# Attention and expert routing on one core: new order of steps in a slot, five experts in two passes, key copies on ScalarE, scatters as units end

One Trainium2 chip, one core. The metric is the device time of one execution in microseconds (us). The kernel before takes 208.21 us (median of 3; 207.79 to 211.42). All stamps below are us from the start of the profiled span of the run named. "Granted clock" is the share of full TensorE clock that the profile records; half clock is a record of 0.50. A clock window is one of the stretches of 3.41 us at whose borders these records change.

## The reference

Attention over 4 batches, 8 heads, 768 tokens and head size 64; three heads are causal, five see four first keys and a window of 64. Its output, 3072 tokens by 512, goes to a layer of 8 experts, of which each token uses one or none:

```python
out = x.copy()
do_compute = x @ w_skip > 0
logits = xc @ w_gate                  # xc = x[do_compute]
e_idx = argmax(logits); gate_w = softmax(logits)[e_idx]
for e in range(8):
    h = maximum(xc[mask] @ w1[e], 0)  # 512 -> 1024
    y[mask] = gate_w * (h @ w2[e])    # 1024 -> 512
out[do_compute] = xc + y
```

## The kernel before

Each batch has six slots. A slot mixes score products of batch b (`C`, `H6`, `X`), transposes of q and k (`T`), the attention product of batch b-1 for 128 tokens (`"o"`), and for earlier tokens the transposes of x and the gate scores (`"x"`). In TensorE's program they stand in this order.

```python
def ready(g):                       # this is "x"
    xt(g - 1)                       # 4 transposes of x, copied to SBUF
    gates(g - 2)                    # 4 products with 9 columns, into av's bank

return (
    (C(0), "x", "o", C(1), T(1)),
    (C(2), "x", "o", T(2), C(3)),
    (C(4), "x", "o", C(5), H6(0)),
    (H6(2), "x", "o", T(3), lambda: after_t(b), H6(4)),
    ...
)
...
    if g in (NT + 1, 2 * NT + 1):   # after the second slot of batches 2 and 3
        routing = route(g - NT - 1) # starts by reading the gate scores in av
```

After the last batch a table of slots is made, and GpSimd gathers the tokens of each expert (`gather`), loads weights and scatters results, all in its program order. Experts 0 to 3 run as two units of up to 128 tokens, in two passes; the others as one unit of up to 256.

```python
FB = 4
units = [(e, (t,)) for t in range(T2) for e in range(FB)]
units += [(e, (0, 1)) for e in range(FB, E)]
for n in range(len(units)):
    ...                             # up product, down product
    if n == FB - 1: load_half(FB + 2, 0)
    elif n == FB:   load_half(FB + 2, 1); load_half(FB + 3, 0)
    elif n > FB:
        if n == FB + 1: load_half(FB + 3, 1)
        scatters()                  # loads first, then the scatters
```

The softmax here doesn't subtract the row's maximum and nothing guards it: scores larger than these inputs give would overflow.

## Time and profile before

| | before |
|---|---|
| time, median | 208.21 us |
| profiled span, mean granted TensorE clock | 204.6 us, 0.95 |
| first gather (end of attention and routing) | 109.52 us |
| from first gather to end of span | 95.1 us |

I split the span at the first gather, because all that follows waits for the slot table. The prediction shows the page's lines and the GpSimd timeline.

### The profile page before, as it was taken

The numbers are of one execution on the slowest core, as the hardware profiler recorded it, in microseconds if no ns is written. First come the engines' busy times: TensorE is split into PE (matmuls) and PEld (weight loads), VectorE is DVE, ScalarE is ACT, GpSimd is POOL, SyncE is SP. The second block draws the span as 40 slices with busy tenths as digits, with TensorE's granted clock in tenths as the row PEclk, the third lists the DMA queues.
The fourth block names the chain that finished last, engine by engine and source line by source line (L and its number), as shares of the span: only waits on it lengthen the run. The fifth ranks groups of instructions, "written<-read, shape, count | busy, mean of one in ns | idle before, by whom it ended". The sixth has DMA issues, their size and how long they took to land. (4 is left out here: it accounts for less than half of the span.)

```text
span 204.6 us, 5665 instructions
## 1 busy us (share of the span) xinstructions
PE 163.1 (80%) x2422; PEld 116.7 (57%) x2422; DVE 111.9 (55%) x282; ACT 83.5 (41%) x116; POOL 85.1 (42%) x105
## 2 busy tenths in 40 slices
PE   5898878967788687886898688959988959999900
PEld 1455556746566565664777558648755727657400
DVE  5888877554957849574683626233345344344410
ACT  2067788855874558746121133212322422232000
POOL 8659711421861218412014801687632451145430
PEclk9999999999999999999669889988999999999985
DMA  5999999999899999999999899999999999942010
GB/s 164 174 172 157 180 196 214 222 181 229 139 182 228 240 216 246 225 190 243 215 235 272 222 171 238 208 302 239 239 258 181 208 210 211 278 155 79 23 67 3
DMA packets 53172, 39.97 MB, mean 195 GB/s; under 512 B 27976, under 2 KB 44360, under 8 KB 53136
## 3 DMA queue, kind: packets, MB, share of 16 engines
q0 software_dynamic: 49136, 32.43, 104.2%
q1 hardware_dynamic: 3728, 6.69, 9.7%
q8 instruction: 21, 0.34, 0.6%
q10 hardware_dynamic: 272, 0.39, 0.5%
q14 instruction: 15, 0.12, 0.2%
HBM read 56.66 MB, written 10.49 MB: 328 GB/s over the span
## 5 line engine op out<-in xcount | busy, mean ns | idle before, releaser
L433 POOL CAST x<-x 128x512 f16<-128x512 f32 x17 | 10.7, 627 | 43.3 <-DVE x L426 37.4
L344 ACT ACTIVATE at<-sps 128x1024 f16<-128x1024 f32 (+1 forms) x24 | 21.7, 918 | 11.6 <-PE sps L333 11.1
L685 POOL DMA_INDIRECT out_dram<-xg,idx x16 | 16.0, 1001 | 24.0 <-DVE xg L748 10.6
L731 PE MATMUL mhp<-mxT,w1t 128*128 128x128 f16 (+1 forms) x320 | 24.4, 238 | 0.7 <-ACT mxT L717 0.7
L731 PEld LDWEIGHTS <-w1t 128*128 128x128 f16 x320 | 22.6, 103 | 3.5 <-issue 1.1
L735 DVE TENSOR_SCALAR ht<-mhp 128x512 f16<-128x512 f32 x16 | 11.1, 691 | 23.3 <-PE mhp L731 20.3
L746 PE MATMUL myp<-w2t,ht 128*128 128x512 f16 x96 | 23.6, 380 | 0.0
L748 DVE SCALAR_TENSOR_TENSOR xg<-myp,tab,xg 128x512 f32<-128x512 f32 x16 | 12.0, 751 | 19.6 <-PE myp L746 18.2
L679 POOL DMA_INDIRECT xg<-out_dram,idg x16 | 16.4, 1025 | 10.5 <-DVE tab L536 4.8
L737 ACT ACTIVATE ht<-mhp 128x512 f16<-128x512 f32 x16 | 9.6, 597 | 26.5 <-PE mhp L731 21.1
L383 ACT ACTIVATE ats<-sps 128x1024 f16<-128x1024 f32 (+1 forms) x16 | 12.3, 808 | 14.6 <-PE sps L374 14.6
L746 PEld LDWEIGHTS <-ht 128*128 128x128 f16 x128 | 12.0, 99 | 10.3
L439 PE MATMUL xps<-ident,x 128*128 128x128 f16 (+1 forms) x96 | 12.9, 263 | 6.0 <-ACT qT L302 2.4
L302 DVE COPY kT<-tps 128x768 f16<-128x768 f16 x16 | 15.2, 951 | 3.5 <-PE tps L296 3.5
L333 PE MATMUL sps<-qT,kT 64*128 64x512 f16 (+3 forms) x96 | 15.1, 308 | 0.0
L328 PE MATMUL sps<-tri,idl 64*128 64x128 f16 x144 | 11.4, 221 | 3.3 <-ACT ats L383 2.7
L717 ACT COPY mxT<-mtp 128x512 f16<-128x512 f16 x11 | 6.2, 587 | 17.7 <-PE mtp L714 16.8
L426 DVE TENSOR_TENSOR x<-av,rec 128x512 f32<-128x512 f32 x18 | 12.5, 692 | 1.4
L349 ACT ACTIVATE at<-sps 128x1024 f16<-128x1024 f32 (+1 forms) x12 | 10.8, 916 | 5.0 <-PE sps L333 4.8
L114 POOL DMA_DIRECT2D va<-in_v_dram x8 | 11.4, 1426 | 2.7 <-DMA va<-in_v_dram 1.2
L446 DVE COPY xT<-xps 128x512 f16<-128x512 f16 x17 | 7.6, 446 | 7.2 <-PE xps L439 7.0
L517 POOL TENSOR_TENSOR mv<-ot,vals 128x192 f32<-128x192 f32 (+1 forms) x4 | 2.5, 618 | 21.7 <-DVE ot L511 21.7
(152 smaller groups left out, 341.5 us busy)
## 6 DMA issues: line engine op xcount, KB each, us to landing
out_dram<-x SPq DMA_DIRECT2D x24, 256.0 KB, 5.8
w1t<-in_moe_w_dram POOLq DMA_DIRECT2D x6, 1024.0 KB
w2t<-in_moe_w_dram POOLq DMA_DIRECT2D x6, 1024.0 KB
va<-in_v_dram POOLq DMA_DIRECT2D x8, 384.0 KB
qin<-in_moe_w_dram POOLq DMA_DIRECT2D x2, 1024.0 KB
kin<-in_moe_w_dram POOLq DMA_DIRECT2D x2, 1024.0 KB
qin<-in_q_dram POOLq DMA_DIRECT2D x2, 768.0 KB
kin<-in_k_dram POOLq DMA_DIRECT2D x2, 768.0 KB
```

The lines of the kernel that those rows point to most:

```text
L114: nc.gpsimd.dma_start(out=y[:, x, :D], in_=vr[b, :, x])
L302: eng(t.rearrange("c (p n) -> c p n", n=NT), ps.rearrange("c n p -> c p n"))
L333: nc.tensor.matmul(ps[:, k, x:x + n], kT[b, pr][rows[i], j * P:(j + 1) * P], qT[b, pr][rows[i], q0:q0 + n], start=False, stop=True, skip_g ...
L344: nc.scalar.activation(both[b][:, :, o:o + w], ps[:, :, :w], ACT.Exp, scale=SCALE)
L383: nc.scalar.activation(both[b, pr][:, :, x0:x1], ps[:, :, :x1 - x0], ACT.Exp, scale=SCALE)
L426: nc.vector.tensor_tensor(x.rearrange("p c t d -> p t c d"), avo[:, :, :, :D], rec.unsqueeze(3).to_broadcast([P, 2, 4, D]), op=ALU.mult)
L439: nc.tensor.matmul(ps[:, s], x[:, s * P:(s + 1) * P], ident if x.dtype == FP16 else ident32, is_transpose=True, start=(s == 0), stop=(s == ...
L679: nc.gpsimd.indirect_dma_start(out=xg[e, t], out_offset=None, in_=out[:n, :], in_offset=bass.IndirectOffsetOnAxis(ap=idg[:, t, e:e + 1], a ...
L685: sc = nc.gpsimd.indirect_dma_start(out=out[:, :], out_offset=bass.IndirectOffsetOnAxis(ap=idx[:, t, e:e + 1], axis=0), in_=xg[e, t], in_o ...
L731: nc.tensor.matmul(hp[:, u], wts[e, 0][:, s, (f0 + u) * P:(f0 + u + 1) * P], xts[n][:, s], start=(s == 0 and u == 0), stop=(s == DS - 1 an ...
L746: nc.tensor.matmul(yp, hts[n][:, f, i * P:(i + 1) * P], wts[e, 1][:, f], start=(f == 0), stop=(f == FS - 1))
L748: nc.vector.scalar_tensor_tensor(xg[e, t], yp, tab[:, t, e, 1:2], xg[e, t], ALU.mult, ALU.add)
```

## The change

The intent: put the transposes and gate scores behind the attention product, so that TensorE does not wait for the casts that they need; take half of the key copies from VectorE; load earlier; do the last gate scores between the first units; take five experts in two passes; scatter as units end. The core of the diff (PSUM pools and the unit loop's head are cut):

```diff
-            eng = nc.scalar.copy if name == "qT" and b else nc.vector.tensor_copy
+            eng = nc.scalar.copy if b and (name == "qT" or pr > 1) else nc.vector.tensor_copy
...
-            (C(0), "x", "o", C(1), T(1)),
-            (C(2), "x", "o", T(2), C(3)),
-            (C(4), "x", "o", C(5), H6(0)),
-            (H6(2), "x", "o", T(3), lambda: after_t(b), H6(4)),
-            (X(1, (0,), 0, S), "x", "o", X(2, pair, 0, 512), V(1, 2, 3), X(2, pair, 512, S)),
+            (C(0), "o", C(1), "x", T(1)),
+            (C(2), "o", T(2), C(3), "x"),
+            (C(4), "o", C(5), "x", H6(0)),
+            (H6(2), "o", T(3), lambda: after_t(b), "x", H6(4)),
+            (X(1, (0,), 0, S), "o", X(2, pair, 0, 512), "x", V(1, 2, 3), X(2, pair, 512, S)),
...
         after_o(b)
+        load()
+        load()
...
-    FB = 4
+    FB = 5
...
+        if n > 2:
+            scatters()
         if n == FB - 1:
+            load_half(FB + 1, 0)
+        elif n == FB:
+            load_half(FB + 1, 1)
             load_half(FB + 2, 0)
-        elif n == FB:
+        elif n == FB + 1:
             load_half(FB + 2, 1)
-            load_half(FB + 3, 0)
-        elif n > FB:
-            if n == FB + 1:
-                load_half(FB + 3, 1)
-            scatters()
```

## The prediction

> **What bounds the kernel now.** Times below are us from the start of the profiled span (204.6 us; the timed runs have a median of 208.21). I read the page first, for the busy shares and the slices:

> ```profile
> PE 163.1 (80%) x2422; PEld 116.7 (57%) x2422; DVE 111.9 (55%) x282; ACT 83.5 (41%) x116; POOL 85.1 (42%) x105
> PEclk9999999999999999999669889988999999999985
> DMA  5999999999899999999999899999999999942010
> q0 software_dynamic: 49136, 32.43, 104.2%
> ```

> PE is busy 80% of the span, but the DMA engines are at nine tenths in nearly every slice up to about 180 us, and nearly all of it is one queue, the one GpSimd fills. So there are two full resources, and the end is set by how they interlock. The clock row has dips (6s and 8s): TensorE ran at half clock at 99-106, 116-120 and 136-140.

> Second, the chain of work that ended last, of which I take the pieces after the routing:

> ```profile
> 136.77 10.04 DMA xg<-out_dram,idg
> 147.11 12.61 DMA xg<-out_dram,idg
> 164.60 16.08 DMA out_dram<-xg,idx
> 187.99 6.92 PE myp L746 x32
> ```

> The last gather is issued at 147.1 and lands at 159.7; the chain then runs through a scatter, and ends with the last products and a tail of 9.7 us (194.9 to 204.6) of last product, scatter and closing. Third, GpSimd's timeline, since it feeds the queue:

> ```profile
> 52.75 2.82 POOL L114 DMA_DIRECT2D va<-in_v_dram  x2
> ...
> 109.52 1.14 POOL L679 DMA_INDIRECT xg<-out_dram,idg  x1 [2.07 <-DVE tab L536]
> ...
> 148.11 0.83 POOL L119 DMA_DIRECT2D w1t<-in_moe_w_dram  x1
> 152.46 0.92 POOL L119 DMA_DIRECT2D w2t<-in_moe_w_dram  x1 [3.52 <-PE mhp L731]
> 153.37 0.76 POOL L119 DMA_DIRECT2D w1t<-in_moe_w_dram  x1
> 156.00 0.89 POOL L119 DMA_DIRECT2D w2t<-in_moe_w_dram  x1 [1.87 <-PE myp L746]
> 160.58 1.07 POOL L685 DMA_INDIRECT out_dram<-xg,idx  x1 [3.70 <-DMA xg<-out_dram,idg]
> ```

> What to see: the weights of experts 6 and 7 (four loads) are issued at 148-156, before the first scatter, and the first scatter waits until the last gather has landed. Sorting the trace's DMA packets by size (the two weight halves have 512 packets of 2048 B and 1024 of 1024 B) gives their landings: 163.9, 168.9, 175.1, 180.1, about 5.1 us each when the queue is full. TensorE needs the last one only at about 191.4, so today the queue has 11 us to spare. Fourth, DVE late in the attention:

> ```profile
> 95.10 0.56 DVE L288 COPY vs<-va 64x1560 f16<-64x1560 f16 x1 [2.62 <-DMA va<-in_v_dram]
> ```

> DVE stood 2.6 us for the last batch's v; 14.35 us later (109.45) the first slot table is ready and the gathers start.

> [...] the scatter at 160.58 holds GpSimd 3.70 us, and nothing behind it in GpSimd's program is issued meanwhile. [...] all weights, gathers and scatters here stand in the one q0 line. [...] after the 2.36 us gap before 135.45 it ran at half clock for about 3.4 us, the granted clock being 0.50 in 137-139.

> **The change, part by part.**
> (1) Slot order, key copies, earlier loads. The PE wait list has 1.6 us and the PEld list 5.4 us for GpSimd's casts (L433) in the attention; putting the transposes later in a slot should remove most of it. Six key copies (0.95 us on DVE) become ScalarE copies (0.80): DVE -5.7, ACT +4.8, both under 75% busy there. But the end of attention hangs on v of the last batch, which stands in a full queue. Packets show that queue empty from 51.6 to about 55.1, because the v load of batch 2 was issued at 52.75 behind two casts. The new loads after a batch put it there at about 48, so the queue runs on, and the last v lands 3.5 us sooner, at 91.6. The routing product that followed it moves behind other work, about 0.6 us. So the table is ready at 91.6 + 14.35 - 0.6 = 105.3 instead of 109.45: 4.1 us won, whatever else attention saves.
> (2) Five gathers instead of four in the first pass: 1.33 us more of GpSimd ahead of the three loads (w2 of 3, w1 and w2 of 4). These took from 117.0 to 136.8 = 19.8. Now: issue at 105.3 + 0.1 + 5 x 1.33 = 112.0, first packets 2.4 later (as from 114.6 to 117.0), landed at 134.2.
> (3) Gate scores between units. From the last attention product (116.3) to the first down product (128.10) before: 11.8 us. After: four transposes of 0.45, two up products of 1.78, gates and rank sums 0.5, two short waits 0.7 = 6.6, plus 1.7 if the half clock of 116-120 stays = 8.3; 1.3 of the old 11.8 is the table product, which moves later. So about 2.2 us won: first down at 120.4 (105.3 + 6.85 + 8.25).
> (4) Second pass: the table product now stands behind three units: 3 downs with a transpose (2.2) and 2 ups (1.78) = 10.15, table 1.8: ready at 132.4, against 128.7 before. The first t=1 gather lands 3.8 after issue (as 109.52 to 113.3), 136.3; TensorE wants it at about 135: a wait of 1-2 us.
> (5) Scatters as units end, and here is the cost. The built program shows that the first scatter still waits for every gather, and that expert 6's first load now stands behind it and four more scatters. From 135 the queue has 11 gathers (1.06 each, from 136.8 to 180.1 = 43.3 less six weights of 5.1, over 12 gathers) and two weights: 21.9, so the last gather lands at 157. First scatter 157.6, five of them at 1.33: 6.6, so w1 of 6 is issued at 164.2 instead of 148.1. The queue is nearly empty from 157 to 166.6. Then four weights at 5.1 plus two scatters (0.6) and 1.5 of skew: w1 of 6 lands at about 172.5, w1 of 7 at 183.6, w2 of 7 at 189.8 (before: 163.9, 175.1, 180.1).
> TensorE from 136.5: half a down 0.9, five units of 4.0, w1 of 5 3.5, one down with transposes 2.3, 0.5 = 27.2: it wants w1 of 6 at 163.7 and waits 8.8 us; its up at half clock takes 5.2, down 4.1, a second wait for w1 of 7 to 183.6, up 3.5 to 5.2, two downs 6.9: products end at 194 to 196. Before: 194.9. The tail of 9.7 is the same.
> Sum: the 4.1 us of (1) and the 2.2 of (3) are spent on the later issue in (5). Span near 204.6, ratio near 1.00.

> **The rivals.**
> A. TensorE sets the end: if the weights were there in time, the products would run on from 163.7 by 3.5 + 4.1 + 3.5 + 6.9 = 18 to 181.7 and the span would be 191.4, about 195 us timed. For it: PE is the busiest engine and all the parts remove its waits. Against: the program order on GpSimd and 5.1 us per weight. A half-way form, the queue draining faster or gathers landing sooner by 4 us, gives about 203.
> B. The attention gains nothing or loses (ScalarE in program order holds the two transposed copies one after the other, PSUM transposes wait for it): the table stays at 109.4, all that follows is 4 us later: 212.
> C. The attention gains more than the v load lets me believe, or w2 of 3, which took 9.7 us with the output writes beside it, goes at 6: 2-3 us better, 205.

> **Range and chances.** The worked sum says 208. Errors of the three chained stages (start of table, landing of gathers, four loads) are some 2 us each, 3.5 together. A and C together look to me somewhat likelier than B, a judgement and not a measurement, so I lean by 1 us: predicted 207.0 us, 202.5 to 211.5 in eight of ten; faster by over 2% 0.26, within 2% 0.60, slower by over 2% 0.14.

> **What would show it.** (1) right: the last v copies start near 91.6 and the first gather near 105.4. (3) right: first down product near 120. (5) right: GpSimd's first scatter waits for a gather to about 157 and w1 of 6 is issued after five scatters near 164; DMA slices near 160-166 fall well under nine; TensorE shows a long wait on the weights of experts 6 and 7 and a half clock there, which the profile of before has nowhere. Wrong if TensorE's up product of expert 6 starts without a wait before 166, or if the first gather starts later than 108.

## More of the kernel before

One more view matters later, the list of what TensorE waits for from 27 to 109 us; its columns are total us, number of waits, longest. The first lines, and the one on the routing:

```profile
PE sps L328 <- ACT ats L383: 2.7, 3, 0.9
PE xps L439 <- ACT qT L302: 2.4, 4, 0.7
...
PE av L451 <- DVE wm L474: 1.4, 2, 0.7
```

TensorE has many short waits, most of them under 1 us; the longest in the list is 1.4 us. `av L451 <- DVE wm` is the gate product waiting until the routing's vector chain has read the gate scores, which lie in the bank it writes.

## The result, and the profile after

The changed kernel takes 227.88 us (median of 4; 226.2 to 229.27) beside 208.59 for the kernel before (median of 4, with one run more): the ratio is 1.0935, 95% interval 1.081 to 1.107. (A ratio is the mean time of one kernel's fast runs over that of the other's of the same rounds, so not quite the ratio of the medians. "Fast" leaves out executions over 1.5% above the fastest of the same kernel.) Slower by 9%, far outside my range.

The page's lines after, to be held against the four that the prediction shows first:

```profile
PE 179.9 (80%) x2448; PEld 126.5 (56%) x2448; DVE 105.5 (47%) x276; ACT 88.3 (39%) x122; POOL 84.9 (38%) x105
PEclk9999999999755769755699669999999999679995
DMA  6999999999999999999412679994899437999820
q0 software_dynamic: 49136, 32.43, 95.7%
```

The transfers are the same to the packet, and TensorE has only 26 instructions more, but 16.8 us more busy time. The clock row says why: from the eleventh slice on (a slice is 5.6 us) it has two holes, `7557` and `7556`, where before it had nines (products of 128 rows and 512 columns start 0.216 us apart at full clock and 0.426 at half). In the clock records: half clock at 58.7-75.8, 79.2-82.6 and 92.9-109.9, in batches 2 and 3. The DMA row falls to 4, 1, 2 at slices 20 to 22: the queue was nearly empty just before the gathers. GpSimd's timeline after:

```profile
49.19 2.82 POOL L114 DMA_DIRECT2D va<-in_v_dram  x2
...
123.43 1.14 POOL L683 DMA_INDIRECT xg<-out_dram,idg  x1 [2.07 <-DVE tab L538]
...
178.81 1.04 POOL L689 DMA_INDIRECT out_dram<-xg,idx  x1 [11.22 <-DMA xg<-out_dram,idg]
...
185.16 0.86 POOL L119 DMA_DIRECT2D w1t<-in_moe_w_dram  x1
```

The first gather starts at 123.43 instead of 109.52, 13.9 us later. From there to the end it is 100.7 us instead of 95.1. So of 19.5 us of span, 13.9 are lost before the slot table and 5.6 after it. The chain that ended last now goes through the weights of the last experts:

```profile
166.60 11.26 DMA xg<-out_dram,idg
...
188.26 15.93 DMA w1t<-in_moe_w_dram
204.24 3.67 PE mhp L735 x32
207.90 6.92 PE myp L750 x32
```

On VectorE, the last copies of v, for which it waited 2.62 us before:

```profile
108.31 0.79 DVE L290 COPY vs<-va 64x1560 f16<-64x1560 f16 x1
```

No wait: the data was there, and VectorE came late. What TensorE waits for from 27 to 123 us, first and fourth line:

```profile
PE av L408 <- DVE wm L476: 2.7, 2, 1.4
...
PE av L453 <- DVE x L428: 1.9, 6, 0.5
```

It is now the attention product of the third slot (L408) that waits for the routing's chain, 1.4 us in each of batches 2 and 3; before, the transposes lay in that place and the wait was 0.7. That is 1.3 us more, a tenth of the loss. For the rest I looked at TensorE's speed. Here are TensorE's clock windows, 3.41 us each, by their times; the first PE figure is its busy time, the granted clock is the third figure from the end:

```profile
core 0: us, PE busy (x) PEld busy (x) DVE busy (x) ACT busy (x) POOL busy (x), PEclk, DMA share, GB/s
51.90:55.32 3.42, 3.10 (x85) 2.46 (x83) 2.50 (x6) 2.96 (x4) 2.31 (x4) 1.00 1.95 210
55.32:58.73 3.41, 1.86 (x41) 1.39 (x35) 1.76 (x9) 3.13 (x5) 2.20 (x3) 1.00 2.15 193
58.73:62.14 3.41, 3.30 (x40) 2.17 (x34) 1.60 (x5) 0.91 (x2) 0.62 (x1) 0.50 1.31 244
...
68.97:72.38 3.41, 3.41 (x41) 2.34 (x41) 1.09 (x7) 1.51 (x2) 0.00 (x0) 0.50 1.18 244
72.38:75.80 3.42, 3.42 (x56) 2.28 (x56) 2.28 (x5) 1.62 (x2) 1.10 (x2) 0.50 1.12 213
75.80:79.21 3.41, 2.47 (x34) 2.19 (x33) 1.96 (x6) 0.70 (x1) 0.00 (x0) 1.00 1.17 238
```

The window with the new wait has 1.86 us of TensorE work; the next five run at half clock, although TensorE is then busy for 3.21 to 3.42 us in four of them (1.78 in that from 65.55).

### The profile page after: what moved, and what is told of

Same layout as the page of the kernel before. It is cut to its first block, busy times and chain, and to the rows that moved or that the text cites. A ratio compares the mean times of both kernels' runs of the same rounds, so it can differ in the third digit from the quotient of the medians.

```text
span 224.1 us, 5717 instructions
## 1 busy us (share of the span) xinstructions
PE 179.9 (80%) x2448; PEld 126.5 (56%) x2448; DVE 105.5 (47%) x276; ACT 88.3 (39%) x122; POOL 84.9 (38%) x105
## 3 DMA queue, kind: packets, MB, share of 16 engines
q0 software_dynamic: 49136, 32.43, 95.7%
## 5 line engine op out<-in xcount | busy, mean ns | idle before, releaser
L435 POOL CAST x<-x 128x512 f16<-128x512 f32 x17 | 10.5, 616 | 59.1 <-DVE x L428 56.9
L735 PE MATMUL mhp<-mxT,w1t 128*128 128x128 f16 (+1 forms) x320 | 25.7, 243 | 6.7 <-DMA w1t<-in_moe_w_dram 4.7
L335 PE MATMUL sps<-qT,kT 64*128 64x512 f16 (+3 forms) x96 | 17.8, 340 | 0.4 <-DVE kT L304 0.4
L385 ACT ACTIVATE ats<-sps 128x1024 f16<-128x1024 f32 (+1 forms) x16 | 12.9, 813 | 12.8 <-PE sps L376 12.7
L750 PEld LDWEIGHTS <-ht 128*128 128x128 f16 x128 | 11.8, 98 | 9.8
L426 DVE RECIPROCAL rec<-av 128x8 f32<-128x8 f32 x18 | 3.7, 207 | 22.9 <-PE av L423 22.9
L330 PE MATMUL sps<-tri,idl 64*128 64x128 f16 x144 | 13.0, 238 | 0.6 <-ACT at L346 0.6
L415 PEld LDWEIGHTS <-at 128*128 128x128 f16 x252 | 11.5, 108 | 1.8 <-issue 1.1
L304 DVE COPY kT<-tps 128x768 f16<-128x768 f16 x10 | 9.5, 953 | 6.1 <-PE tps L298 6.1
L284 PE MATMUL av<-esk,ident 128*128 128x512 f16 x28 | 10.1, 492 | 2.6 <-DVE ident L142 1.8
```

The lines of the kernel that those rows point to most:

```text
L330: nc.tensor.matmul(ps[:, k, x:x + P], idl[rows[i], u], tri[rows[i], u], start=(u == 0), stop=False, skip_group_check=True)
L335: nc.tensor.matmul(ps[:, k, x:x + n], kT[b, pr][rows[i], j * P:(j + 1) * P], qT[b, pr][rows[i], q0:q0 + n], start=False, stop=True, skip_g ...
L385: nc.scalar.activation(both[b, pr][:, :, x0:x1], ps[:, :, :x1 - x0], ACT.Exp, scale=SCALE)
L415: nc.tensor.matmul(avo[:, 0, h // 2], at[b, h][:, x0:x0 + P], va[b % 2][:, h, j], start=False, stop=j == i, skip_group_check=True)
L735: nc.tensor.matmul(hp[:, u], wts[e, 0][:, s, (f0 + u) * P:(f0 + u + 1) * P], xts[n][:, s], start=(s == 0 and u == 0), stop=(s == DS - 1 an ...
L750: nc.tensor.matmul(yp, hts[n][:, f, i * P:(i + 1) * P], wts[e, 1][:, f], start=(f == 0), stop=(f == FS - 1))
```

## The theories

A. The new order makes one clock window light; TensorE falls to half clock, then needs so long for its work that it stays there for some 17 us, in batches 2 and 3. B. The clock only accompanies it: the order and its waits cost the time. C. Other parts cost it (key copies on ScalarE, PSUM pools, five gathers). For the second half, D: the scatters ahead of the weight loads hold them back.

The runs went out on several chips on which the kernel before took medians of 200.5 to 207.5 us. Kernels are compared only within the same rounds. Times in the headings are medians of 4 or 5. The profiles of experiments 5, 6, 9, 10 and 13 are of runs that count as slow, so their stamps and half-clock sums are those of a slow run.

## The experiments

**1. Second and third slot in the old order** (219.18 us)

```diff
-            (C(2), "o", T(2), C(3), "x"),
-            (C(4), "o", C(5), "x", H6(0)),
+            (C(2), "x", "o", T(2), C(3)),
+            (C(4), "x", "o", C(5), H6(0)),
```

> The changed kernel, with only slots 1 and 2 of each batch (where the routing of the batch before is begun) put back in the old order: transposes and gate scores ahead of the attention product. Clock theory (the product of slot 2 waits 1.4 us for the first routing chain, [...] and the attention then crawls at half clock for 17 us, in batches 2 and 3): the half clock at 59-76 and 93-110 is gone, the first slot table is ready at 107-111 instead of 123.2, and the time falls by 11 to 15 us to 212-216. Rival, ScalarE's key copies are what slows the attention: no change of the clock rows, 226. Rival, the reordering of the other slots or the later transposes of the next batch: under 4 us gained.

The fast runs have a mean of 217.1 beside 205.0 for before, 1.06. Before the first gather, now at 111.45, only one window of 3.4 us runs at half. Its clock row:

```profile
PEclk9999999999999889999988589996999996589995
```

Two slots hold nearly all of the first half's loss: 12.0 of 13.9 us. The time still missed the 212 to 216 that I expected, mainly because the second part took 104.1 us here, 3.5 more than in the kernel after.

**2. Key copies back on VectorE** (228.25 us)

```diff
-            eng = nc.scalar.copy if b and (name == "qT" or pr > 1) else nc.vector.tensor_copy
+            eng = nc.scalar.copy if name == "qT" and b else nc.vector.tensor_copy
```

> The changed kernel with all key copies back on DVE. Key-copy theory: attention back at its old pace, first slot table at 107-111, time 212-216. Clock theory: the wait of slot 2 for the routing chain stays at about 1.4 us, the half clock stays in at least one of the two stretches, and the time stays at 222-229.

Ratio 1.110 (1.096 to 1.124), first gather at 124.14. They are not the cause.

**3. Routing reads a copy of the scores** (225.37 us)

```diff
-        lx = lg[:, cs]
+        lx = mk("lc", [P, n, E + 1])
+        nc.vector.tensor_copy(lx, lg[:, cs])
```

> The changed kernel, in its own slot order, but each routing first copies its gate scores from PSUM to SBUF in one DVE instruction and works on the copy, so that the product of slot 2 waits for one instruction (about 0.25 us) instead of the fifth (1.1 us). Clock theory: the wait shrinks from 1.4 to about 0.5 us, the low window disappears and with it the half clock of 17 us twice; first table at 105-111, time 210-216. If the order of the slots itself is to blame and not the wait, the gain is under 3 us. Other theories: 226.

Ratio 1.097 (1.088 to 1.106), first gather at 121.81. The wait of L408 shrank to 0.9 us in two, but 37.5 us before the first gather still ran at half clock, as in the kernel after. So taking the one long wait away does not bring the clock back, and the time stays where the clock stays. Some of the wait only moved: the gate product's wait for VectorE's `x` (L453) rose from 1.9 to 3.5 us. A part of theory A, that this wait alone is the trigger, fell here; by what I expected, the order of the slots is to blame.

**4. Weight loads ahead of the scatters** (223.12 us)

```diff
-        if n > 2:
-            scatters()
...
+        elif n > FB:
+            if n == FB + 1:
+                load_half(FB + 2, 1)
+            scatters()
```

> The changed kernel with the weight loads of experts 6 and 7 issued ahead of the first scatter, as before the change; nothing else. Theory of the recorded prediction for the second half: the attention stays slow (first table at 123), but w1 of expert 6 is issued some 15 us earlier, TensorE's 4.7 us wait for it and the half clock after it go, and the time falls by 4 to 8 us to 218-222. If the loads are not what holds the second half, under 2 us.

Ratio 1.088 (1.080 to 1.096). First gather at 122.67, and 98.1 us from there to the end, where the kernel after has 100.7 and experiments 2 and 3 have 101.6 and 101.8. The half clock near 190 us is gone. Theory D holds, at some 3 us, less than the 4 to 8 that I expected.

**5. Five idle products in the wait** (215.63 us), a direct test of A against B: nothing is reordered, TensorE only gets something to do.

```diff
-            (C(4), "o", C(5), "x", H6(0)),
+            (C(4), lambda: b > 1 and fills(5, tp.tile([P, 512], FP32, tag="t", name="fps")), "o", C(5), "x", H6(0)),
```

> The kernel after with five idle products of 128x512 on TensorE ahead of the attention product of the third slot of batches 2 and 3, where TensorE waits 1.37 us for the routing's vector chain. They move no data that is used and remove no wait; they only keep TensorE at work. Theory A (the reorder lowers TensorE's activity in one clock window and the clock then stays at half for some 17 us in each of the two batches, which is the 14 us lost before the first slot table): the long half-clock stretches near 59 to 76 and 93 to 110 us go or shrink to one window of 3.4 us, the first gather comes 8 to 13 us earlier than 123.4 us, time 214 to 220. Theory B (the clock is only a companion; the added wait for VectorE and the order of the steps cost the time themselves): first gather within 2 us of 123.4, time 225 to 229.

Ratio 1.066 (1.055 to 1.076). Batch 3 lost its half-clock stretch, batch 2 kept one of 13.7 us; the first gather came at 116.17, 7.3 us earlier. That is half of A's claim.

**6. The new order alone, in the kernel before** (217.25 us): the six slot lines of the diff above and nothing else.

> The kernel before with only the order of the steps in a slot taken from the changed one; four experts in the first pass, the second half and the key copies as before. Theory A (the reorder alone costs the first half its clock): half-clock stretches of about 17 us in batches 2 and 3, first gather 10 to 15 us later than 109.5 us, time 217 to 223, ratio about 1.05 to 1.07. Rival C (only the mix of reorder and the other parts, for example key copies or the PSUM pools, costs it): first gather within 3 us of 109.5, time within 2% of before.

Ratio 1.069 (1.055 to 1.083). In its profile 44 us before the first gather run at half, and GpSimd starts it here:

```profile
125.14 1.14 POOL L679 DMA_INDIRECT xg<-out_dram,idg  x1 [2.08 <-DVE tab L536]
```

This profile is of a slow run, but the fast runs agree: their mean is 214.5 beside 200.5, a loss of 14.0 us with the second part of the kernel before. The order alone makes the whole loss of the first half; rival C falls.

**7. Experiments 1 and 4 together** (213.21 us).

> The kernel after with both repairs: second and third slot in the old order, and the loads of the last weights ahead of the first scatter. If the two losses are separate (about 9 us and about 4.5 us, as measured one at a time), time 213 to 216 and first gather near 111.5; if they overlap, 216 to 219. A time at or under 208 would mean that the rest of the change gains, which nothing measured so far says.

Ratio 1.066 (1.057 to 1.076). Here 17 us of half clock came back before the first gather (116.09), with the same attention program as in experiment 1. The windows' borders lie elsewhere in each trace (one at 98.90 in the kernel before, at 97.16 and 100.57 in experiment 8; at 72.38 in the kernel after, at 73.5 in experiment 15). That this decides which windows turn light is my guess; no run tests it. The second part took 92.2 us. As a sum of two effects this run is inconclusive.

**8. Idle products in the kernel before** (204.95 us), at the last slot's wait for a vector result.

```diff
-            (lambda: sinks(b), "x", "o", X(3, pair, 0, 512), go_on, X(3, pair, 512, S)),
+            (lambda: sinks(b), "x", "o", X(3, pair, 0, 512),
+             lambda: fills(5, tp.tile([P, 512], FP32, tag="t", name="fps")), go_on,
+             X(3, pair, 512, S)),
```

> The kernel before with five idle products of 128x512 in the last slot of batch 3, where TensorE waits 1.42 us for a vector result at 96.0 us and the two clock windows that follow, 98.9 to 105.7 us, run at half. Theory A (too little work in one window costs the clock of the next): no half clock at 98.9 to 105.7, first gather 1.5 to 3.5 us earlier than 109.5, time 1 to 3 us below the kernel before of the same call, so same within 2%. If the clock follows no such rule: half clock stays, time unchanged or up to 1 us longer.

A miss: 100.6 to 107.4 us still ran at half clock, first gather at 109.37, and the two fast runs (mean 201.7) are no better than before (200.5). In the trace the five products run from 94.70 to 95.95, in the clock window before the one (97.16 to 100.57) that half clock followed. So the products missed that window, and the run tests neither answer.

**9. All six slots in the old order, loads first** (203.54 us): the kernel after without the two suspects.

> The kernel after with the old order in all six slots and the loads of the last weights ahead of the first scatter: five experts, gates between their first units, key copies on ScalarE and the two extra loads of each batch stay. If the order of the slots and the scatters ahead of the loads are the whole loss: first gather within 3 us of that of the kernel before (109.5 us in its trace), time within 2% of before in the same call, ratio 0.98 to 1.02. If something else in the change costs as well (five gathers, key copies, other PSUM pools): ratio 1.02 to 1.05. Under 0.98 would be a version that beats both; I give that one chance in ten.

Ratio 1.014 (1.007 to 1.020). The profiled run is a slow one, with a clock of 0.916; the four fast runs have 0.954 to 0.967, as before has. In the slow one 22.7 us before the first gather (113.52) ran at half: the old order can lose the clock too. So all the rest of the change, five experts and gates between units included, gains nothing and costs about 1.4%.

**10. Seventeen idle products a batch** (220.0 us).

```diff
-            (C(4), "o", C(5), "x", H6(0)),
-            (H6(2), "o", T(3), lambda: after_t(b), "x", H6(4)),
+            (C(4), keep(5), "o", C(5), keep(4), "x", keep(4), H6(0)),
+            (H6(2), keep(4), "o", T(3), lambda: after_t(b), "x", H6(4)),
```

> The kernel after, whole order kept, with idle products of 128x512 at four places of the third and fourth slot of batches 2 and 3 (17 in each batch, some 3.6 us of TensorE's time at full clock, of which about 1.9 us lies in waits). With five of them the stretch in batch 3 went and that in batch 2 stayed[...]. Theory A: both long half-clock stretches before 110 us are gone or one window long, first gather 110 to 114, ratio to before of the same call 1.03 to 1.06, below the 1.066 with five. If the clock is not the cause: the added work makes it longer than with five, ratio over 1.07, first gather later than 117.

Ratio 1.095 (1.087 to 1.103): what B expected. But half clock before the first gather fell to 19 us, and the gather, at 121.79, is later than that amount of half clock explains by about 7 us. An idle product takes 0.216 us at full clock (the distance of two starts in the trace), so 34 of them are 7.3 us; that most of it did not lie in waits is my reading, not a measurement. The run mixes a gain and a cost, and needed a cleaner one.

**11. Half of the key copies moved, in the kernel before** (201.58 us): experiment 2's edit reversed, on the kernel before.

> The kernel before with only half of the key copies moved from VectorE to ScalarE. Putting them back in the changed kernel changed nothing over 1%, so here the time stays within 2% of before, ratio 0.985 to 1.015, first gather within 2 us of 109.5, and no new half-clock stretch before 95 us. If ScalarE is the tighter engine in the attention part: first gather 3 us or more later and waits of TensorE for ScalarE's copies up by as much.

Ratio 1.002 (0.995 to 1.010), first gather at 108.39. No effect.

**12. Idle products only in waits** (213.45 us)

```diff
-            (C(4), "o", C(5), "x", H6(0)),
+            (C(4), keep(5), "o", C(5), keep(3), "x", H6(0)),
```

> The kernel after with five idle products of 128x512 in the wait ahead of the attention product of the third slot and three in the next wait of that slot (0.48 us, for VectorE's x), in batches 2 and 3, 16 in all and nearly all in time that TensorE would wait. Over the twelve profiles that do without such products, the start of the first gather follows 107.3 us + 0.40 x (time at half clock before it) within 3 us; the one with 34 idle products came 7.2 us above it, which is their own time. Theory A: the stretch near 60 to 75 us of batch 2 shortens to 7 us or less, that of batch 3 stays away, the first gather comes at 110 to 115, ratio to before 1.04 to 1.06. Theory B (order and waits, not the clock): first gather 116 or later even where under 8 us of half clock precede it, ratio 1.07 or more.

(The line of 0.40 was fitted to ten profiles, not twelve as I wrote; with all twelve that have no idle products it is 107.6 + 0.38 x, the largest miss 2.8 us.) This is the decisive run. TensorE's timeline in the third slot of batch 2, first of the kernel after, then of this one:

```profile
56.25 0.38 PE L335 MATMUL sps<-qT,kT 64*128 64x512 f16 x2
57.99 0.27 PE L408 MATMUL av<-vsk,esk 128*128 128x260 f16 x1 [1.37 <-DVE wm L476]
```

```profile
56.23 0.38 PE L335 MATMUL sps<-qT,kT 64*128 64x512 f16 x2
56.54 1.25 PE L284 MATMUL fps<-esk,ident 128*128 128x512 f16 x5
57.98 0.27 PE L408 MATMUL av<-vsk,esk 128*128 128x260 f16 x1 [0.18 <-DVE wm L476]
```

The attention product starts at the same moment, 57.98 against 57.99; nothing on the path was made shorter. And the clock row is whole until the gathers:

```profile
PEclk9999999999999999999997999999999995599995
```

No window before the first gather ran at half, and that gather came at 112.95: 10.5 us earlier than in the kernel after, with 16 products of useless work added. Theory B's claim, 116 or later, falls. What is left to 109.52 is 3.4 us of order, waits and idle products; and as 6.8 us before the gather of the kernel before ran at half, at like clock it is more: this run lies 5.3 us above the line. The ratio is 1.064 (1.049 to 1.079), just above what I expected, because the second part still takes 97.6 us. In the list of TensorE's waits after the first gather:

```profile
PE mhp L737 <- DMA w1t<-in_moe_w_dram: 9.3, 2, 8.8
```

With TensorE at full clock the wait for expert 6's weights is 8.8 us; in the kernel after it was 4.7, since TensorE itself was later.

**13. Only the second and third slot in the new order, in the kernel before** (210.8 us); **14. only the third** (212.38 us).

```diff
-            (C(2), "x", "o", T(2), C(3)),          # 13 only
-            (C(4), "x", "o", C(5), H6(0)),         # 13 and 14
+            (C(2), "o", T(2), C(3), "x"),
+            (C(4), "o", C(5), "x", H6(0)),
```

> The kernel before with only the second and third slot in the new order. Theory A, in its form that these two slots hold the light clock window: long half-clock stretches in batches 2 and 3, first gather 5 to 12 us later than 109.5, ratio 1.03 to 1.06. If all six slots together are needed: first gather within 3 us, ratio within 1.02.

> The kernel before with only the third slot in the new order, the slot whose attention product then waits 1.4 us for the routing's vector chain. If this one wait is enough to lose the clock: a half-clock stretch of 10 to 17 us in batches 2 and 3, ratio 1.03 to 1.06. If the neighbouring slot's order is needed as well (its transposes at its end): at most one or two short windows at half, first gather within 3 us of 109.5, ratio under 1.02. I put these at even chances.

Two slots: ratio 1.042 (1.020 to 1.064); in the profile, of a slow run, 41 us of half clock before the first gather at 120.62. One slot: no clear answer. Its profiled run took 202.41 us at a mean clock of 0.954, the other three 210.0 to 214.9 at 0.879 to 0.905. The same program is quick or slow by up to 6% according to its clock. Three of the four count as slow, so I draw no size from it.

**15. Both repairs, order kept** (210.7 us): experiment 12's idle products and experiment 4's loads.

> The kernel after, its whole order of steps kept, with the two repairs that the runs so far point to: the idle products in the waits of the third slot (16 in all), and the loads of the last weights ahead of the first scatter. With the idle products alone no window before the first gather ran at half, the gather came at 112.95, and the rest took 97.7 us, with TensorE waiting for the weights of expert 6; with the loads first the rest took 92.2 to 98.1 us in two profiles. If these two are the whole loss and add up: span 205 to 208, ratio to before of the same call 1.02 to 1.04, no half clock between 170 and 195. If the second half is slow for another reason: ratio 1.05 or more.

The two fast runs have a mean of 208.6 beside 202.5 for before, 1.03, as expected; no half clock between 111 and 196 us, and 92.2 us from the first gather to the end. But before the first gather (114.46) half clock came back for 13.7 us (73.5-76.9, 94.0-100.8, 107.7-111.1), with the attention program of experiment 12, which had none:

```profile
PEclk9999999999999969995797999999999999999955
```

So these 16 products keep the clock in one execution and only partly in another. The 92.2 us are no gain over the kernel before either: the five profiles that keep its second part (experiments 6, 8, 11, 13 and 14) need 90.6 to 92.0 for it, less than the 95.1 of its own trace. GpSimd now issues the weights first:

```profile
155.41 0.80 POOL L119 DMA_DIRECT2D w1t<-in_moe_w_dram  x1 [1.15 <-DMA qin<-in_moe_w_dram]
...
169.30 1.07 POOL L691 DMA_INDIRECT out_dram<-xg,idx  x1 [6.06 <-DMA xg<-out_dram,idg]
```

The two repairs together take the loss from 9% to 3% without undoing the order. No version beat the kernel before.

## What makes a window light

Busy time does not separate the windows well: in experiment 3 one with 2.64 us of busy TensorE was followed by half clock, while in the kernel before one with 2.07 was not. From the trace I summed for every window of 30 to 125 us, in all 17 profiles, the columns streamed by its matmuls, times active rows / 128, times 4 for 32-bit data (the 4 is my choice and not measured: in the kernel after 32-bit transposes of 128 columns (L718) start 0.109 us apart at full clock, 16-bit ones 0.056, which is a factor of 2). Idle products of 512 columns start 0.216 us apart, so a full window at full clock holds about 8,090 of these units (3.413 / 0.216 x 512). It is no upper bound: products of 64 rows and 64 columns can start at the same moment (two at 69.71 in the kernel after), and the fullest window has 9,557 units. Windows counted by the clock of the *next* one:

| units in a window | at full clock: next half / next full | units | at half clock: next half / next full |
|---|---|---|---|
| under 3,100 | 11 / 0 | under 3,500 | 46 / 0 |
| 3,100 to 4,200 | 26 / 22 | 3,500 to 4,300 | 16 / 3 |
| 4,200 to 4,700 | 7 / 19 | 4,300 to 4,600 | 3 / 6 |
| over 4,700 | 5 / 268 | over 4,600 | 4 / 38 |

## Why the prediction was wrong

- **Step (1), the failed one**: "the table is ready at 91.6 + 14.35 - 0.6 = 105.3 instead of 109.45: 4.1 us won, whatever else attention saves". The first gather came at 123.43. I let the load of v set the end and kept TensorE's speed. The load did go out earlier (49.19), as I said, and the wait for v was gone. But the reorder cost TensorE its clock: experiment 12, which gave the clock back, brought the gather 10.5 us earlier. And even at full clock the gain did not come: there the last v copies start at 97.61 with no wait for a transfer, not at 91.6. Once v no longer held VectorE, I take it that the order of the steps did; no run tests that.
- **Its reason**: I counted 7.0 us of waits for GpSimd's casts as removable, without asking what the moved transposes had been doing where they stood: they filled the time of the routing's chain. I read the clock row as a record of the past and gave the clock no place among the rivals of the first half. Rival B named "the attention gains nothing or loses", but stopped at 4 us and at ScalarE.
- **Step (2)**: landing of w2 of 4, predicted 28.8 us after the first gather starts (105.4 to 134.2), measured 29.0 (152.4 in the packet records). Right.
- **Step (3)**: first down product predicted 15.1 us after the table, measured 15.6 (138.97). Right.
- **Step (4)**: second table 27.1 after the first predicted, 28.1 measured (151.43), and a wait of 1.8 us for the first gather of the second pass, as said. Right, with luck in it: the 4.68 us in which VectorE stood here (last section) were not foreseen, and experiments 5, 7, 9, 10, 12 and 15, without it, have 23.8 to 25.2 us.
- **Step (5)**: the first scatter 52.3 us after the table predicted, 55.4 measured; expert 6's load 58.9 predicted, 61.8 measured, behind five scatters, as said. The wait of 8.8 us was 4.7, and 8.8 once TensorE had its clock (experiment 12). With the loads first the second part is shorter by some 3 us (experiment 4) and, with TensorE at full clock, by 5.4 (97.6 in experiment 12, 92.2 in 15, on two chips). Right in mechanism and near in size, but not in the sum: it was to be paid for by the gain of step (1).
- **The sum**: from table to end I had 99.3 us, measured 100.7. My own sign "wrong if the first gather starts later than 108" is what happened. The range held only the errors of three stages and no change of speed, so it was too narrow.
- I had looked for windows in which TensorE was idle throughout. Even the gap of 2.36 us before 135.45, after which the kernel before ran at half clock from 136.45 to 139.86, is shorter than a window. There was no idle window: the longest single gap inside any of the 49 windows that led to half clock, in all profiles up to 125 us, is 1.97 us.

Open: why the single new slot (experiment 14) loses the clock in some executions and not in others is only guessed at, from where the windows' borders fall; and of the 1.4% left in experiment 9 I know only that key copies are not in it.

## What to carry to other kernels

Before moving a step on TensorE, ask what runs in the gap that it leaves: sum the work of each clock window, not only the waits, and treat a window that falls well below its neighbours as a possible loss of several windows (here 1.86 us of work after a window with 3.10, then five windows at half clock). Idle products placed in waits are a quick test and a partial cure, and the cure can differ between executions (no half clock before the first gather in experiment 12, 13.7 us of it in 15); outside waits they add work (34 x 0.216 = 7.3 us in experiment 10, an estimate). Loads that a later stage waits for belong ahead of scatters that wait for something themselves (worth some 3 us in experiment 4).

## What else the traces show, and what stays open

- In the 17 profiles 49 windows before 125 us led to half clock, with at least 1.28 us of busy TensorE in each and no gap over 1.97 us; in the fit the border lay near half of 8,090 units.
- One busy window did not always bring full clock back. In the kernel after TensorE was busy 3.30 of 3.41 us (58.73 to 62.14) and 3.41 (68.97 to 72.38) and stayed at half, while after 79.21 to 82.62, also busy 3.41, it was back (busy time by the profile, whose ends are modelled); in the fit, it came back after 44 of the 51 half-clock windows of over 4,300 units, and after 3 of the 65 below.
- Transposes: in the fit above, leaving them out misplaces 42 of 358 full-clock windows at the best border, counting them like other products 24; with a factor of 2 or 1 for 32-bit data, or without the weighting by rows, leaving them out was worse too. A fit, not a separate test.
- A stand without a cause: in the kernel after, VectorE stood 4.68 us until 130.75 while GpSimd issued gathers, put down to no engine of the core; in experiments 1 to 4 it was 4.63 to 4.67 us. Experiments 5, 7, 9, 10, 12 and 15 issue the same five gathers without it, so it is not the gathers alone. The cause stays open.
